# Reloads and values tied to TensorE, a third buffer for weight pieces, and a last tile in halves, in an attention and two-MoE kernel

## The chip, the cores and the metric

The kernel runs on one core of a Trainium2 chip. TensorE (PE) multiplies, VectorE (DVE) and ScalarE (ACT) work on elements, GpSimd (POOL) issues some transfers, and SyncE (SP) issues most of them, one after another in program order. The metric is the device time of one execution in microseconds (us), as the median of several executions.

## What is computed

```python
p_packed = sm_attn(p, k, v)            # 4 batches, 8 heads, 32 packed rows, 576 positions, 64 wide
out = sm_attn(q, p_packed, p_packed)   # softmax(scale * q @ k.T) @ v, the sum with 1e-9
x = out as 2304 tokens x 512
x = mish(x @ moe_w_in) @ moe_w_out     # 512 -> 2048 -> 512
x = elu(x @ moe2_w_in) @ moe2_w_out    # 512 -> 2048 -> 512
```

All data is f32. q, k and p are drawn eight times larger than v.

## The kernel before, in words

The matrix products run on pairs: a value is split into a high part (`gh`, `w1oh`) and the rest (`gl`, `w1ol`), and three products (high-high, high-low, low-high) make one. ACT writes the high part (`split_hi`), DVE the low part (`split_lo`).

**Startup** (`startup`, to about 125 us) takes the attention of batches 0 and 1 and the first 32 of the first MoE's 128 steps; its order is written out by hand in the string ORDER, for all engines. Behind it the framework's scheduler orders the instructions of each engine by priorities and its own estimate of times, within what the dependencies allow.

**`mixture1`** runs a loop over i = 32 to 129, a step per block of 288 tokens and 128 of the 2048 inner columns. Each step makes `gemm1(i)` (6 matmuls of 288 columns into a bank `h`), `mish(i)` on ACT and DVE, and `gemm2(i - 2)` (12 matmuls into `acc`). Between these the next batches advance in small steps from two queues: `att` (attention of batches 2 and 3: keys transposed on DVE, scores of the two halves s = 0 and 1 by `scores1`, softmax, transposes of the exponentials by `transpose_a1`, product with v by `packed`) and `fol`, the folds. `fold(b, c)` multiplies the first MoE's input weight, a quarter c, into the packed attention of batch b, so that batch b's `gemm1` needs no attention output. The decoded weight lies in DRAM (`w1_dr`, 8 pieces of 512 KB) and is read back by `reload_w1i(c)` into two tiles `w1r`c`_`h, five steps before the fold is due. Third, `step_w2` cuts the second MoE's input weight: raw words are loaded (`raw_w2i`), decoded by one step on ACT (L201) and three on DVE (L221, L231, L237), summed and differenced, and seven combined pieces `w2c` are split by ACT and DVE and written to DRAM by POOL (L326). They come back later for `mixture2`.

Two resources matter. PSUM's pool `ps_p` has one pair of banks, `pm`: after the startup each fold, each half of the scores and each transpose takes it in turn, and frees it when ACT and DVE have read it. And SP's transfers use eight semaphores in turn: a transfer of SP is issued only when the one eight places before it has landed.

**`mixture2`** runs three blocks j of 768 tokens. `quartet(j, q)` makes seven products of y and w2c in place of eight (p0 to p6, L833), with sums in `hs` and `r` on ACT and DVE and elu; `gemm4` adds up the second product in six banks (L913 to L915). `second(c)` and `tick(n)` feed the loads and decode of `w2o` into the same loop, n steps at a time.

`behind(ins)` puts an instruction after the last DVE instruction recorded so far, in the scheduler's order only (NoSync: nothing waits on the chip). The lines that the change touches: pool `wo` L109, `behind` L148, `reload_w1i` L336 to L343, `load_heads` L353, `transpose_a1` L495, `gemm4` L904, `attention_steps` L947, `second` L1113, `whole` L1137, the tick in `mixture2` L1262.

Of the kernel before, what the change touches and what calls it, by code (L numbers as in the profile page):

```python
# [72 lines left out]
def kernel(  # L73
# [32 lines left out]
    ptp = ctx.enter_context(tc.tile_pool(name="ptp", bufs=2))  # L106
    st = ctx.enter_context(tc.tile_pool(name="st", bufs=3))
    sg = ctx.enter_context(tc.tile_pool(name="sg", bufs=2))
    wo = ctx.enter_context(tc.tile_pool(name="wo", bufs=2))  # L109
    ps_a = ctx.enter_context(tc.tile_pool(name="ps_a", bufs=2, space=bass.MemoryType.PSUM))  # L110
    ps_h = ctx.enter_context(tc.tile_pool(name="ps_h", bufs=2, space=bass.MemoryType.PSUM))
    ps_p = ctx.enter_context(tc.tile_pool(name="ps_p", bufs=1, space=bass.MemoryType.PSUM))
# [32 lines left out]

    raws, halves, words = {}, {}, (deque(), deque())

    def behind(ins):  # L148
        last = next(
            (i for i in reversed(nc.cur_bb.bb.instructions) if i.engine == nc.vector.engine), None  # L150
        )
        if last is not None:
            tc.add_manual_dep(
                ins.ins, last.name,
                mybir.DependencyInfo(mybir.DependencyClass.NoSync, mybir.DependencyReason.DATA),
                reason="plan",
            )

# [178 lines left out]
    def reload_w1i(c, *which):  # L337
        for h in which or range(2):
            t = slot([128, 2, 512], F32, f"w1r{c}_{h}")
            ins = nc.sync.dma_start(out=t, in_=w1_dr[c * 2 + h])  # L340
            if which:
                behind(ins)
            w1v[c, h] = t  # L343


# [8 lines left out]
    def load_heads(src, dst, b, g, nm, eng):  # L354
        home = small if b else slot
        if nm == "v":
            t = home([128, 2, 5, D], F32, f"{nm}{b}_{g}")
            x = src[b, 2 * g:2 * g + 2].rearrange("h (p i) d -> p h (i d)", i=9)
            for r, j, n in RUNS:
                (eng if b or not j else nc.scalar).dma_start(  # L360
                    out=t[r:r + 64, :, 0:n, :].rearrange("p h i d -> p h (i d)"),
                    in_=x[:, :, D * j:D * (j + n)],
                )
        elif b == 0 or nm == "k" and b == 1:

            t = home([128, S // 32, 32], F32, f"{nm}{b}_{g}")
            ins = eng.dma_start(
                out=t.rearrange("p c d -> p (c d)"),
                in_=src[b, 2 * g:2 * g + 2].rearrange("h (t j) d -> (h t) (j d)", t=64),
            )  # L370
            if b == 1:
                tc.keep_in_program_order(ins)
        else:
            t = home([128, S // 32, 32], F32, f"{nm}{b}_{g}")
            for h in range(2):
                for x in range(2):
                    r = 64 * h + 32 * x
                    if nm == "q":
                        eng.dma_start(
                            out=t[r:r + 32],  # L380
                            in_=src[b, 2 * g + h, :, 32 * x:32 * x + 32].rearrange("(c t) d -> t c d", t=32),
                        )
                    for s in range(2 if nm == "k" else 0):
                        eng.dma_start(
                            out=t[r:r + 32, s * NB // 2:(s + 1) * NB // 2, :],
                            in_=src[b, 2 * g + s, h * HALF:(h + 1) * HALF, 32 * x:32 * x + 32].rearrange(
                                "(c t) d -> t c d", t=32
                            ),
                        )
        dst[b, g] = t  # L390
# [96 lines left out]
    def transpose_a1(b, s, eng):  # L487
        d = {}

        def pe():  # L490
            e1 = E1.pop((b, s))
            ps = d["ps"] = pm()
            for i, w, bank, x in CHUNKS:
                i0 = i * 128
                nc.tensor.transpose(  # L495
                    out=ps[bank][0:w, x * 128:(x + 1) * 128], in_=e1[:, i0:i0 + w], identity=ident
                )

        def post(eng=eng):
            a1 = small([128, len(CHUNKS), 128], F32, f"a1t{b}_{s}")  # L500
            for bank in range(2):
                mine = [c for c in CHUNKS if c[2] == bank]
                w, i0, n = mine[0][1], mine[0][0], len(mine)
                evac(
                    eng, a1[0:w, i0:i0 + n, :],
                    d["ps"][bank][0:w, 0:n * 128].rearrange("p (c x) -> p c x", x=128),
                )
            A1T[b, s] = a1

        return [pe, post]  # L510
# [391 lines left out]
    def gemm4(j, kk, half):  # L902
# [4 lines left out]
        gh, gl = gt2.pop((j, kk, half))  # L907
        wh, wl = (x[:, kk % 2, :] for x in wt["w2o", kk // 2])
        n = count[j, half] = count.get((j, half), 0) + 1
        for t in range(3):  # L910
            ts = slice(t * 128, (t + 1) * 128)
            o = acc[j][3 * half + t]
            nc.tensor.matmul(out=o, lhsT=gh[:, ts], rhs=wh, start=(n == 1), stop=False)  # L913
            nc.tensor.matmul(out=o, lhsT=gh[:, ts], rhs=wl, start=False, stop=False)  # L914
            nc.tensor.matmul(out=o, lhsT=gl[:, ts], rhs=wh, start=False, stop=(n == NK))  # L915
        if n == NK:
            for t in range(3):
                o = acc[j][3 * half + t]
# [4 lines left out]
                else:  # L923
                    ob = slot([128, 512], F32, "ob")
                eng = nc.gpsimd if j < 2 else (nc.sync, nc.scalar)[t % 2]
                evac("av"[t % 2], ob, o)
                a = 2 * HN * j + HN * half + t * 128

                r = 0
                while r < 128 and a + r < S:  # L930
# [16 lines left out]
    def attention_steps(b):  # L947
# [9 lines left out]
        st = [transpose_heads(kt_in, kT, b, g, "kT") for g in range(4)]  # L957
        for s in range(2):
            pe, top, expo, sums = scores1(b, s)
            st.append([then(pe, lambda: load_vt(b, 0), lambda: load_vt(b, 1)) if s else pe, lambda top=top, expo=expo: (top(), expo()), sums])  # L960
        st += [transpose_a1(b, s, P["EVA"][s]) for s in range(2)]
        for s in range(2):
            pe, scaled, turn, out = packed(b, s)
            st.append([then(pe, lambda s=s: load_kt(q, qt_in, b, s, "q")), scaled, lambda turn=turn, out=out: (turn(), out())])
# [20 lines left out]
    def startup():  # L985
# [15 lines left out]
        if WARM:  # L1001
            wu = ps_h.tile([128, 512], F32, tag="h", name="warm")

            one = const.tile([128, 128], F32R, name="one")
            nc.gpsimd.tensor_copy(out=one, in_=ident)

            def busy():
# [104 lines left out]

    def second(c):  # L1113
        rows = [4 * c + r for r in (0, 2, 1, 3)]
        for r in rows[:2]:
            todo.append(lambda r=r: load_raw("w2o", r, 0))
        for x, r in enumerate(rows):
            d = []

            def step(i, r=r, d=d):  # L1120
                if not d:
                    d.extend(decode("w2o", r, 0))
                d[i]()

            todo.extend(lambda i=i, step=step: step(i) for i in range(6))
            if x < 2:
                todo.append(lambda r=rows[x + 2]: load_raw("w2o", r, 0))

    def tick(n):
        while n and todo:  # L1130
# [3 lines left out]
    def mixture1():  # L1134
        att, fol = Track(), Track()

        def whole(f):  # L1137
            return [f[0], lambda: [f[i]() for i in (1, 3, 2, 4)]]

        at = {}  # L1140

# [93 lines left out]
    def mixture2():  # L1235
        ready = deque()
        for j in range(3):
            for q in range(NQ):
# [13 lines left out]
                for x in range(7):  # L1252
# [4 lines left out]
                    if x in (0, 2, 4, 6):  # L1257
                        if x == 6:
                            ready.append(groups[0])
                        if ready:  # L1260
                            gemm4(*ready.popleft())
                    tick(4 if lastq else 2)  # L1262
                ready.extend(groups[1:])
        while ready:
            gemm4(*ready.popleft())
# [37 lines left out]
```

## Time and profile before

| | |
|---|---|
| runs | 778.14, 778.45 and 782.45 us, median 778.45 |
| profiled execution | 775.32 us, of which the span from the first to the last instruction is 773.5 |
| busy | PE 756.9 us (98%), DVE 528.7 (68%), ACT 397.6 (51%), POOL 104.5 (14%) |
| DMA | 138.82 MB, 179 GB/s on average |
| largest groups | L833 198.1 us, L737 to L739 148.7 to 151.2 each, L913 to L915 101.1 to 113.5 each, all PE |

A matmul's busy time overlaps that of its neighbour, so a PE that is busy without a gap issues a 288-column matmul every 0.13 us though each is shown with 0.29. Line numbers are those of the kernel before; after the change they are two to five higher in the functions named here, and more from `gemm4` on.

### The profile page before, as it was taken

The numbers are of one execution on the slowest core, as the hardware profiler recorded it, in microseconds if no ns is written. First come the engines' busy times: TensorE is split into PE (matmuls) and PEld (weight loads), VectorE is DVE, ScalarE is ACT, GpSimd is POOL, SyncE is SP. The second block draws the span as 40 slices with busy tenths as digits, with TensorE's granted clock in tenths as the row PEclk, the third lists the DMA queues.
The fourth block names the chain that finished last, engine by engine and source line by source line (L and its number), as shares of the span: only waits on it lengthen the run. The fifth ranks groups of instructions, "written<-read, shape, count | busy, mean of one in ns | idle before, by whom it ended". The sixth has DMA issues, their size and how long they took to land.

```text
span 773.5 us, 14181 instructions
## 1 busy us (share of the span) xinstructions
PE 756.9 (98%) x5276; PEld 679.0 (88%) x5276; DVE 528.7 (68%) x1132; ACT 397.6 (51%) x843; POOL 104.5 (14%) x199
## 2 busy tenths in 40 slices
PE   8899999999999999999999999999999999999997
PEld 6598898898889988999988889888998999899986
DVE  5999977735853679877667788866455686445554
ACT  3899826573657467665545344534323354223323
POOL 1100000120120215661000003133000001000000
PEclk9999999999999999999999999999999999999999
DMA  8998646685583555777666235456343347333312
GB/s 290 412 367 271 171 126 177 203 230 157 129 268 56 151 194 191 262 254 238 219 220 201 100 109 199 155 197 198 108 120 119 103 140 243 108 110 116 129 55 82
DMA packets 95108, 138.82 MB, mean 179 GB/s; under 512 B 57920, under 2 KB 63616, under 8 KB 95040
## 3 DMA queue, kind: packets, MB, share of 16 engines
q1 hardware_dynamic: 83104, 105.73, 44.1%
q0 software_dynamic: 10208, 29.90, 10.6%
q10 hardware_dynamic: 1728, 2.29, 0.9%
q8 instruction: 42, 0.69, 0.3%
q14 instruction: 26, 0.21, 0.1%
HBM read 109.58 MB, written 28.31 MB: 178 GB/s over the span
## 4 chain that ended last, share of the span: by engine, by line
PE 84%; ACT 6%; DVE 4%; DMA 3%; issue 2%; POOL 0%; SPq 0%; ACTq 0%; DVEq 0%; POOLq 0%
PE h L833 22%; PE o L913 8%; PE o L915 8%; PE o L914 8%; PE acc L738 7%; PE acc L737 7%; PE acc L739 7%; PE h L701 3%; PE h L702 3%; PE h L703 3%; DMA raw_w1o<-in_moe_w_out_dram 1%; PE pm L667 1%; PE pm L520 1%; DMA w_dr<-w2c 1%; ACT words L206 1%
## 5 line engine op out<-in xcount | busy, mean ns | idle before, releaser
L833 PE MATMUL h<-y,w2c 128*128 128x384 f32 x1008 | 198.1, 338 | 1.8 <-ACT hs L397 1.2
L833 PEld LDWEIGHTS h<-y,w2c 128*128 128x128 f32 x1008 | 179.5, 188 | 13.4 <-ACT hs L397 2.0
L738 PE MATMUL acc<-gl,w1oh 128*128 128x288 f32 x512 | 151.2, 296 | 0.4 <-DVE gl L719 0.3
L739 PE MATMUL acc<-gh,w1ol 128*128 128x288 f32 x512 | 150.3, 295 | 0.0
L737 PE MATMUL acc<-gh,w1oh 128*128 128x288 f32 x512 | 148.7, 296 | 0.2 <-ACT gh L397 0.2
L913 PE MATMUL o<-w2oh,gh 128*128 128x512 f32 x288 | 113.5, 394 | 0.0
L914 PE MATMUL o<-w2ol,gh 128*128 128x512 f32 x288 | 112.6, 391 | 0.0
L915 PE MATMUL o<-w2oh,gl 128*128 128x512 f32 x288 | 101.1, 393 | 0.0
L738 PEld LDWEIGHTS acc<-gl,w1oh 128*128 128x128 f32 x512 | 96.1, 188 | 5.3 <-issue 2.3
L737 PEld LDWEIGHTS acc<-gh,w1oh 128*128 128x128 f32 x512 | 95.0, 188 | 6.2 <-issue 4.5
L739 PEld LDWEIGHTS acc<-gh,w1ol 128*128 128x128 f32 x512 | 96.0, 188 | 1.2 <-issue 0.8
L719 DVE TENSOR_TENSOR gl<-t,gh 128x288 fp32r<-128x288 f32 x128 | 57.2, 451 | 43.3 <-ACT gh L397 42.4
L711 ACT ACTIVATE t<-h 128x288 f32<-128x288 f32 x128 | 51.0, 404 | 55.9 <-PE h L703 53.0
L701 PE MATMUL h<-a2h,gh 128*128 128x288 f32 x256 | 76.9, 301 | 1.3 <-ACT t L711 0.9
L326 POOL DMA_DIRECT2D w_dr<-w2c x112 | 59.7, 539 | 135.7 <-DVE w2c L272 126.9
L703 PE MATMUL h<-a2h,gl 128*128 128x288 f32 x256 | 76.1, 298 | 0.3 <-DVE gl L272 0.3
L702 PE MATMUL h<-a2l,gh 128*128 128x288 f32 x256 | 75.8, 296 | 0.0
L264 ACT ACTIVATE gh<-t 128x384 fp32r<-128x384 f32 x96 | 50.1, 522 | 48.8 <-DVE t L844 47.5
L270 DVE TENSOR_TENSOR gl<-t,gh 128x384 fp32r<-128x384 f32 x96 | 53.1, 554 | 15.8 <-ACT gh L264 15.4
L914 PEld LDWEIGHTS o<-w2ol,gh 128*128 128x128 f32 x288 | 54.1, 188 | 9.4
L913 PEld LDWEIGHTS o<-w2oh,gh 128*128 128x128 f32 x288 | 54.0, 187 | 9.4 <-ACT gh L264 0.5
L397 ACT ACTIVATE gh<-t 128x288 fp32r<-128x288 f32 x112 | 49.2, 442 | 24.1 <-PE acc L739 22.1
(139 smaller groups left out, 1095.2 us busy)
## 6 DMA issues: line engine op xcount, KB each, us to landing
w2c<-w_dr SPq DMA_DIRECT2D x84, 512.0 KB, 3.6
w_dr<-w2c POOLq DMA_DIRECT2D x112, 128.0 KB, 3.1
w1r<-w_dr SPq DMA_DIRECT2D x24, 512.0 KB, 5.7
raw_w1i<-in_moe_w_in_dram SPq DMA_DIRECT2D x16, 512.0 KB, 10.8
raw_w1o<-in_moe_w_out_dram SPq DMA_DIRECT2D x16, 512.0 KB, 9.1
raw_w2i<-in_moe_w_in_dram SPq DMA_DIRECT2D x16, 512.0 KB, 4.8
raw_w2o<-in_moe_w_out_dram SPq DMA_DIRECT2D x16, 512.0 KB, 3.6
y_dr<-y POOLq DMA_DIRECT2D x16, 288.0 KB, 4.9
```

What stands on the lines that cost most here:

```text
L326: nc.gpsimd.dma_start(out=w2_dr[n // 2][:, n % 2, p], in_=d[x][:, i].bitcast(F32))
L701: nc.tensor.matmul(out=hp, lhsT=wh, rhs=xh, start=(kt == 0), stop=False)
L702: nc.tensor.matmul(out=hp, lhsT=wh, rhs=xl, start=False, stop=False)
L703: nc.tensor.matmul(out=hp, lhsT=wl, rhs=xh, start=False, stop=(kt == 1))
L719: nc.vector.tensor_tensor(out=gl, in0=d["t"], in1=gh.bitcast(F32), op=ALU.subtract)
L737: nc.tensor.matmul(out=o, lhsT=wh[:, cs], rhs=gh, start=first, stop=False)
L738: nc.tensor.matmul(out=o, lhsT=wh[:, cs], rhs=gl, start=False, stop=False)
L739: nc.tensor.matmul(out=o, lhsT=wl[:, cs], rhs=gh, start=False, stop=last)
L833: nc.tensor.matmul(out=hp, lhsT=w[:, p, a, :], rhs=y[:, b, :], start=start and p == 0 and i == 0, stop=p == 1 and i == 2, skip_group_check ...
L913: nc.tensor.matmul(out=o, lhsT=gh[:, ts], rhs=wh, start=(n == 1), stop=False)
L914: nc.tensor.matmul(out=o, lhsT=gh[:, ts], rhs=wl, start=False, stop=False)
L915: nc.tensor.matmul(out=o, lhsT=gl[:, ts], rhs=wh, start=False, stop=(n == NK))
```

## The change

1. The pool `wo` (pieces `w2c` while they are written out, and `r` of `quartet`) has three buffers.
2. `behind` takes an engine and can make a real wait. A reload of `mixture1` (called without `which`) waits on the chip for the last PE instruction recorded; so do the eight loads of v of each of the batches 2 and 3.
3. v is loaded in two parts, one behind the scores of each half. Transposes of half 1 of the batches 2 and 3 stand behind the last PE instruction in the scheduler's order, and for batch 2 half 0 gets three empty steps.
4. The fold's copies run high, high, low, low (before: high, low, high, low).
5. The tile `one` of the startup comes from another pool.
6. `second` loads w2o two decode steps earlier and the next group's first rows ahead; `tick` takes three steps instead of two in the quartets 0 to 5 of the first block.
7. The last output tile is multiplied, copied and stored in two halves of 256 columns.

```diff
     sg = ctx.enter_context(tc.tile_pool(name="sg", bufs=2))
-    wo = ctx.enter_context(tc.tile_pool(name="wo", bufs=2))
+    wo = ctx.enter_context(tc.tile_pool(name="wo", bufs=3))
...

-    def behind(ins):
+    def behind(ins, eng=nc.vector, wait=False):
         last = next(
-            (i for i in reversed(nc.cur_bb.bb.instructions) if i.engine == nc.vector.engine), None
+            (i for i in reversed(nc.cur_bb.bb.instructions) if i.engine == eng.engine and i.name != ins.ins.name), None
         )
         if last is not None:
             tc.add_manual_dep(
                 ins.ins, last.name,
-                mybir.DependencyInfo(mybir.DependencyClass.NoSync, mybir.DependencyReason.DATA),
+                mybir.DependencyInfo(
+                    mybir.DependencyClass.Sync if wait else mybir.DependencyClass.NoSync, mybir.DependencyReason.DATA
+                ),
                 reason="plan",
             )

...
         for h in which or range(2):
             t = slot([128, 2, 512], F32, f"w1r{c}_{h}")
             ins = nc.sync.dma_start(out=t, in_=w1_dr[c * 2 + h])
-            if which:
-                behind(ins)
+            behind(ins, nc.vector if which else nc.tensor, not which)
...
             t = home([128, 2, 5, D], F32, f"{nm}{b}_{g}")
             x = src[b, 2 * g:2 * g + 2].rearrange("h (p i) d -> p h (i d)", i=9)
             for r, j, n in RUNS:
-                (eng if b or not j else nc.scalar).dma_start(
+                ins = (eng if b or not j else nc.scalar).dma_start(
                     out=t[r:r + 64, :, 0:n, :].rearrange("p h i d -> p h (i d)"),
                     in_=x[:, :, D * j:D * (j + n)],
                 )
+                if b > 1:
+                    behind(ins, nc.tensor, True)
...
             ps = d["ps"] = pm()
             for i, w, bank, x in CHUNKS:
                 i0 = i * 128
-                nc.tensor.transpose(
+                ins = nc.tensor.transpose(
                     out=ps[bank][0:w, x * 128:(x + 1) * 128], in_=e1[:, i0:i0 + w], identity=ident
                 )
+                if b > 1 and s and not i:
+                    behind(ins, nc.tensor)
...
         n = count[j, half] = count.get((j, half), 0) + 1
+
+        def products(t, cs, skip):
+            ts = slice(t * 128, (t + 1) * 128)
+            o = acc[j][3 * half + t][:, cs]
+            nc.tensor.matmul(out=o, lhsT=gh[:, ts], rhs=wh[:, cs], start=(n == 1), stop=False, skip_group_check=skip)
+            nc.tensor.matmul(out=o, lhsT=gh[:, ts], rhs=wl[:, cs], start=False, stop=False, skip_group_check=skip)
+            nc.tensor.matmul(out=o, lhsT=gl[:, ts], rhs=wh[:, cs], start=False, stop=(n == NK), skip_group_check=skip)
+
+        final = n == NK and j == 2 and not half
+        cuts = [slice(0, 256), slice(256, 512)]
         for t in range(3):
-            ts = slice(t * 128, (t + 1) * 128)
-            o = acc[j][3 * half + t]
-            nc.tensor.matmul(out=o, lhsT=gh[:, ts], rhs=wh, start=(n == 1), stop=False)
-            nc.tensor.matmul(out=o, lhsT=gh[:, ts], rhs=wl, start=False, stop=False)
-            nc.tensor.matmul(out=o, lhsT=gl[:, ts], rhs=wh, start=False, stop=(n == NK))
+            for cs in cuts if final and t == 2 else [slice(0, 512)]:
+                products(t, cs, cs.start is not None and cs.start > 0)
         if n == NK:
             for t in range(3):
                 o = acc[j][3 * half + t]
...
                 else:
                     ob = slot([128, 512], F32, "ob")
                 eng = nc.gpsimd if j < 2 else (nc.sync, nc.scalar)[t % 2]
+                a = 2 * HN * j + HN * half + t * 128
+                if final and t == 2:
+                    for x, cs in enumerate(cuts):
+                        evac("av"[x], ob[:, cs], o[:, cs])
+                        (nc.scalar, nc.sync)[x].dma_start(out=out[a:a + 128, cs], in_=ob[:, cs])
+                    continue
                 evac("av"[t % 2], ob, o)
-                a = 2 * HN * j + HN * half + t * 128
...
         st = [transpose_heads(kt_in, kT, b, g, "kT") for g in range(4)]
         for s in range(2):
             pe, top, expo, sums = scores1(b, s)
-            st.append([then(pe, lambda: load_vt(b, 0), lambda: load_vt(b, 1)) if s else pe, lambda top=top, expo=expo: (top(), expo()), sums])
+            st.append([then(pe, lambda s=s: load_vt(b, s)), lambda top=top, expo=expo: (top(), expo()), sums])
         st += [transpose_a1(b, s, P["EVA"][s]) for s in range(2)]
+        if b == 2:
+            st[-2] += [lambda: None] * 3
         for s in range(2):
...
-            one = const.tile([128, 128], F32R, name="one")
+            one = tp.tile([128, HN], F32R, tag="t", name="one")[:, 0:128]
...

     def second(c):
         rows = [4 * c + r for r in (0, 2, 1, 3)]
-        for r in rows[:2]:
+        ahead = rows[2:] + [r + 4 for r in rows[:2] if 0 < c < 3]
+        for r in rows[:2 if c < 2 else 0]:
             todo.append(lambda r=r: load_raw("w2o", r, 0))
         for x, r in enumerate(rows):
             d = []
...
                     d.extend(decode("w2o", r, 0))
                 d[i]()

-            todo.extend(lambda i=i, step=step: step(i) for i in range(6))
-            if x < 2:
-                todo.append(lambda r=rows[x + 2]: load_raw("w2o", r, 0))
+            todo.extend(lambda i=i, step=step: step(i) for i in range(4))
+            for n in ahead[x:x + 1]:
+                todo.append(lambda n=n: load_raw("w2o", n, 0))
+            todo.extend(lambda i=i, step=step: step(i) for i in range(4, 6))

...
         att, fol = Track(), Track()

         def whole(f):
-            return [f[0], lambda: [f[i]() for i in (1, 3, 2, 4)]]
+            return [f[0], lambda: [g() for g in f[1:]]]

...
-                    tick(4 if lastq else 2)
+                    tick(4 if lastq else 3 if j == 0 and q < 6 else 2)
```

Where rows move, three places. SP's queue at the end of the startup (k2 are the keys of batch 2, w1r1 to w1r3 the reloads for batch 1's folds, raw_w2i the second MoE's first rows), before:

```order
L384 DMA k2_0_1930<-in_k_dram 32x9x32 x6
L340 DMA w1r1_0_1918<-w1_dr2_141 128x1024
L340 DMA w1r1_1_1920<-w1_dr3_142 128x1024
L340 DMA w1r2_0_1922<-w1_dr4_143 128x1024
L340 DMA w1r2_1_1924<-w1_dr5_144 128x1024
L340 DMA w1r3_0_1926<-w1_dr6_145 128x1024
L340 DMA w1r3_1_1928<-w1_dr7_146 128x1024
L384 DMA k2_0_1930<-in_k_dram 32x9x32 x2
L384 DMA k2_1_1939<-in_k_dram 32x9x32 x8
L384 DMA k2_2_1948<-in_k_dram 32x9x32 x8
L384 DMA k2_3_1957<-in_k_dram 32x9x32 x8
L162 DMA raw_w2i0_0_2000<-in_moe2_w_in_dram 128x1024
```

And after:

```order
L387 DMA k2_0_1930<-in_k_dram 32x9x32 x8
L342 DMA w1r1_0_1918<-w1_dr2_141 128x1024
L342 DMA w1r1_1_1920<-w1_dr3_142 128x1024
L342 DMA w1r2_0_1922<-w1_dr4_143 128x1024
L342 DMA w1r2_1_1924<-w1_dr5_144 128x1024
L342 DMA w1r3_0_1926<-w1_dr6_145 128x1024
L342 DMA w1r3_1_1928<-w1_dr7_146 128x1024
L387 DMA k2_1_1939<-in_k_dram 32x9x32 x8
L387 DMA k2_2_1948<-in_k_dram 32x9x32 x8
L387 DMA k2_3_1957<-in_k_dram 32x9x32 x8
L164 DMA raw_w2i0_0_2000<-in_moe2_w_in_dram 128x1024
```

Two k2 loads moved ahead of the reloads; 24 stand behind them, and now behind the reloads' wait on PE. Further on, four loads of v2 moved ahead of the fourth w2i row and the next reloads.

On DVE, between the keys' transposes and the maximum of the scores of batch 2, half 0 (`gl1_3` is the low part of the last fold of batch 1, `dec` the decoding of raw_w2i), before:

```order
L272 SCALAR_TENSOR_TENSOR w2c_2369<-dec_2051,w2c_2369 128x2x128
L237 SCALAR_TENSOR_TENSOR dec_2187<-raw_w2i1_0_2002,dec_2187 128x512
L289 TENSOR_TENSOR sums_2285<-dec_2051,dec_2187 128x256
L272 SCALAR_TENSOR_TENSOR gl1_3_2098<-pm_2059,gh1_3_2097 128x512
L289 TENSOR_TENSOR sums_2285<-sums_2285,dec_2051 128x256
L289 TENSOR_TENSOR dec_2051<-dec_2051 128x256
L272 SCALAR_TENSOR_TENSOR gl1_3_2098<-pm_2059,gh1_3_2097 128x512
```

And after:

```order
L223 TENSOR_SCALAR dec_2051<-raw_w2i0_0_2000 128x512
L233 SCALAR_TENSOR_TENSOR dec_2051<-raw_w2i0_0_2000,dec_2051 128x512
L223 TENSOR_SCALAR dec_2187<-raw_w2i1_0_2002 128x512
L239 SCALAR_TENSOR_TENSOR dec_2051<-raw_w2i0_0_2000,dec_2051 128x512
L233 SCALAR_TENSOR_TENSOR dec_2187<-raw_w2i1_0_2002,dec_2187 128x512
L274 SCALAR_TENSOR_TENSOR gl1_3_2098<-pm_2059,gh1_3_2097 128x512 x2
L274 SCALAR_TENSOR_TENSOR w2c_2369<-dec_2051,w2c_2369 128x2x128
```

`gl1_3` moved ahead of the pieces and sums, and stands directly behind five decoding steps. ACT has the same picture: its steps on raw_w2i0 and raw_w2i1 (L203) stand directly ahead of the two copies `gh1_3`.

On PE the scores of batch 2, half 0, and what stands around them, before (they begin at PE's row 908):

```order
L701 MATMUL h1_2344<-a2h1_1885,gh1_2_2053 128x288
L431 MATMUL pm_2243<-kT2_3_2215,pD_102 32x288 x2
L431 MATMUL pm_2243<-kT2_2_2185,pD_102 32x288 x2
L431 MATMUL pm_2243<-kT2_1_2157,pD_102 32x288 x2
L431 MATMUL pm_2243<-kT2_0_2128,pD_102 32x288 x2
```

And after (from row 891):

```order
L707 MATMUL h1_2297<-a2l1_1886,gh1_2_2053 128x288
L434 MATMUL pm_2243<-kT2_3_2215,pD_102 32x288 x2
L434 MATMUL pm_2243<-kT2_2_2185,pD_102 32x288 x2
L434 MATMUL pm_2243<-kT2_1_2157,pD_102 32x288 x2
L434 MATMUL pm_2243<-kT2_0_2128,pD_102 32x288 x2
```

They moved 17 rows towards the front, from the gemm1 that makes `h1_2344` into the one before it; the scores of half 1 moved by as many. The fold with w1r1 moved from row 763 to row 769.

## Rows read from the trace of the kernel before

**Rows 1.** The page's first part: span; an engine's busy us, share, instructions.

```profile
span 773.5 us, 14181 instructions
PE 756.9 (98%) x5276; PEld 679.0 (88%) x5276; DVE 528.7 (68%) x1132; ACT 397.6 (51%) x843; POOL 104.5 (14%) x199
```

**Rows 2.** PE's waits, 100 us to the end: line, releaser, us, times, longest.

```profile
PE h L833 <- ACT hs L397: 1.2, 2, 0.6
PE pm L495 <- ACT e L468: 0.5, 1, 0.5
PE h L833 <- DVE t L844: 0.4, 1, 0.4
PE acc L738 <- DVE gl L719: 0.3, 1, 0.3
PE h L833 <- DVE r L895: 0.2, 1, 0.2
PE acc L737 <- ACT gh L397: 0.2, 1, 0.2
```

**Rows 3.** Windows: length; PE, PEld, DVE, ACT, POOL busy; clock; DMA; GB/s.

```profile
20.00:40.00 20.00, 16.05 (x97) 11.04 (x96) 19.55 (x46) 16.59 (x31) 2.73 (x4) 1.00 1.02 412
...
150.00:170.00 20.00, 19.47 (x169) 17.99 (x168) 8.73 (x25) 14.64 (x32) 6.41 (x12) 1.00 0.92 283
```

**Rows 4.** Timeline of SP's queue: start us, us, engine, line, transfer, count.

```profile
111.10 12.08 SPq L340 DMA_DIRECT2D w1r<-w_dr  x6
123.23 14.31 SPq L384 DMA_DIRECT2D k<-in_k_dram  x26
137.66 10.06 SPq L162 DMA_DIRECT2D raw_w2i<-in_moe_w_in_dram  x4
150.77 9.02 SPq L360 DMA_DIRECT2D v<-in_v_dram  x8
```

**Rows 5.** Line L340, the reloads: ns to issue (min/median/max); time to landing.

```profile
L340 SPq DMA_DIRECT2D w1r<-w_dr x24: 319/380/1078, 46.1 to 282.7; - x24
...
DMA to landing us min/median/max: 3.2/5.7/9.7
```

**Rows 6.** Timeline of PE, five places (start, length, matmuls run together).

```profile
124.63 0.29 PE L703 MATMUL h<-a2h,gl 128*128 128x288 f32 x1
...
130.39 1.09 PE L667 MATMUL pm<-w1r,pt 64*32 64x512 f32 x16
...
152.34 0.71 PE L431 MATMUL pm<-kT,pD 64*32 64x288 f32 x16
...
158.45 0.72 PE L431 MATMUL pm<-kT,pD 64*32 64x288 f32 x16
...
173.28 0.90 PE L520 MATMUL pm<-v,a1t 128*32 128x64 f32 x40
```

**Rows 7.** Timeline of ACT around the first w2i rows and the softmax.

```profile
141.84 0.68 ACT L201 ACTIVATE raw_w2i<-raw_w2i 128x512 f32<-128x512 f32 x1 [0.43 <-DMA raw_w2i<-in_moe_w_in_dram]
...
148.41 0.60 ACT L264 ACTIVATE gh<-pm 128x512 fp32r<-128x512 f32 x1 [1.39 <-DVE gl L272]
...
154.85 1.28 ACT L468 ACT_TABLE_LOAD   x1
...
156.66 0.47 ACT L468 ACTIVATE e<-pm,sm 128x256 f32<-128x256 f32 x1
```

**Rows 8.** Timeline of DVE in the same stretch.

```profile
143.02 0.69 DVE L231 SCALAR_TENSOR_TENSOR dec<-raw_w2i,dec 128x512 int32<-128x512 int32 x1
...
149.04 0.69 DVE L272 SCALAR_TENSOR_TENSOR gl<-pm,gh 128x512 fp32r<-128x512 f32 x1
...
153.16 0.76 DVE L455 TENSOR_REDUCE sm<-pm 128x1 f32<-128x576 f32 x1 [1.05 <-PE pm L431]
```

**Rows 9.** Page, DMA issues: transfer, queue, count, size, median us to landing.

```profile
w_dr<-w2c POOLq DMA_DIRECT2D x112, 128.0 KB, 3.1
```

**Rows 10.** Timeline of DVE at the end of the span.

```profile
768.92 0.69 DVE L399 COPY ob<-o 128x512 f32<-128x512 f32 x1 [1.55 <-ACT ob L397]
```

## The prediction

> **What bounds the kernel now.** I read the page's first part, then the waits of TensorE (PE) after the startup, then the windows, and last the timelines of SP, PE, ACT and DVE around 110 to 165 us. The page says that PE is busy 756.9 of 773.5 us [rows 1]. The reader should see in the waits that after 100 us PE waits for a named releaser only seven times, 2.8 us together, and never longer than 0.6 us at once [rows 2]. So no edit after the startup can win more than about 2.8 us (0.36%), while an edit that makes PE wait costs its full length. The startup is written out by hand and the diff leaves its order alone, so I count nothing before 108 us. One window shows slack that is not there elsewhere: 150 to 170 us has PE at 19.47 of 20.00 [rows 3]. There the scores of batch 2 share one PSUM pair (`pm`) with the last fold of batch 1, and it is the stretch that the new waits reach first.
>
> **The gate on the reloads.** In before, SP issued six reloads of w1 (512 KB each) from 111.10 us, then 26 loads of k2, then the first w2i rows at 137.66 [rows 4]. Now the first reload waits for the last PE instruction recorded ahead of it, the last matmul of `gemm1(31)`, L703 at 124.63 + 0.29 [rows 6]; call it 125.0. Behind it on SP stand the other reloads, 24 k2 loads, and raw_w2i0 and 1. A reload takes SP 0.38 us to issue and lands after 3.2 us at best, 5.7 at the median, 9.7 at worst [rows 5]. Six together are 3.15 MB. At the best rate a window shows, 412 GB/s [rows 3], each takes 1.27 us of the engines: the first lands at 128.2, the second at 129.5, the sixth at 134.6. The first fold that reads them stood at 130.39 [rows 6], and six matmuls later now (131.2), so it does not wait, with 1.7 us to spare.
>
> The Trainium skill, "DMA: Bandwidth & Descriptors", section Specifications, gives a core about 358 GB/s of HBM; by it each reload would take 1.46 us, the sixth would land at 135.5, and the sum below would be 0.9 us larger; the trace's 412 GB/s decides. The Trainium skill, the same page, section Rules for kernel authors, says to issue a DMA early and to wait for it late; that speaks against a gate like this one, and by it the loss that follows is the price.
>
> Each DMA of SP waits for the one eight before it. So the third to eighth load of k2_1 go out as reloads one to six land, the last at 134.6. Sixteen k loads are left, at 14.31/26 = 0.55 us each [rows 4]: they end at 143.4, 5.9 us later than before. raw_w2i0 goes out at 143.5. From its issue to ACT's first touch took 137.66 to 141.84, 4.2 us [rows 4, 7]: now 147.7. raw_w2i1 follows 0.4 us behind and, by the same engine time of 1.3 us, lands near 148.7.
>
> **First stall.** The order now puts ACT's step on raw_w2i1 ahead of both `gh1_3` copies, and DVE's five decode steps ahead of both `gl1_3`. In before they stood beside data that had landed. ACT: 148.7 + 0.68 = 149.4, then two copies of 0.60 [rows 7] to 150.5. DVE: 147.7 + 0.68 on ACT, then five steps of 0.4 to 0.69 [rows 8], 2.7 together, to 151.1; then two `gl` of 0.69 to 152.35. Only then is `pm` free. PE wants it for the scores of half 0, which stand 17 rows (0.133 us each) ahead of where they stood: 152.34 - 2.26 = 150.1 [rows 6]. **PE waits 2.2 us.** Bounds: nothing, if all six reloads land as the quickest one did (125.0 + 5 x 0.42 + 3.2 = 130.3, which moves all of this 4.3 us earlier); 4.4 us, if the last takes 9.7 (127.1 + 9.7 = 136.8). I take the value between because six in a row can't each have the engines alone, and nothing stands ahead of them; by the median alone the sixth would land at 127.1 + 5.7 = 132.8 and the stall be 0.4.
>
> **Second stall.** After `gl1_3` DVE has ten steps of about 0.4 us (four of them of w2c, three sums) before the maximum of half 0 (0.76 [rows 8]): 152.35 + 4.0 + 0.8 = 157.1, with the scaling 157.5. ACT has a fourth w2c piece ahead of the table load, and three buffers: it waits for the first piece's write, issued near 153.3, median 3.1 us to land [rows 9]: 156.4. Then three ACT steps (1.2), the table load 1.28, two exponentials (0.98) [rows 7]: 159.9. PE wants `pm` for half 1 at 158.45 - 2.26 + 2.2 = 158.4 [rows 6]. **PE waits 1.5 us.** Bounds: 0.5 if the write is not what ends last (DVE's 157.5, a softmax step already loaded, 0.4 + 0.98 to 158.9); nothing if the sixth reload comes 3.8 us earlier, since all of this hangs on `gl1_3`; 3.0 if the write lands 1.5 us late. The 0.5 that PE waits now at L495 [rows 2] I leave as it is.
>
> **The clock.** PE idled 4 of 20 us between 20 and 40 us and the granted clock stayed 1.00 [rows 3], so the stalls cost their own length.
>
> **Values behind PE.** The eight loads of v2 start at 150.77 [rows 4]. Four now wait for the scores of half 0 and four for those of half 1, near 152.8 and 159. Queued behind them on SP are a raw_w2i row, two reloads and q2. Their first reader, the product with v, stands at 173.28 [rows 6], 13 us after the last issue, longer than the slowest reload took to land [rows 5]. Cost nothing; if that cover went, a microsecond or two, which I put into the upper end. Batch 3 is the same with no stall near it. The transposes tied behind PE and the three empty steps move work that PE does anyway: nothing.
>
> **Fold copies together.** ACT's second copy waited 1.39 us for DVE's `gl` of the first [rows 7]; now ACT runs both and DVE follows. It shortens the hold of `pm` by about 0.9 us per fold, and is already inside the PE order that I use (scores 17 rows earlier). It buys nothing by itself where PE did not wait.
>
> **Third buffer, w2o two steps earlier, three ticks.** These act from 360 us on, where PE's waits are hs 1.2 (two), t 0.4 and r 0.2 [rows 2]. The third buffer also serves `r`; steps of the decode leave DVE and ACT at other times. Which waits go can't be read from the rows: the most is 1.8 us, the least nothing, and a new wait of one step (0.6) is as possible. I take the wait for r and one of the two for hs: **-0.8 us**.
>
> **Tail.** The last tile is copied by ACT and DVE in halves. But the copy that ends last is another one: DVE's copy of 768.92, which waited 1.55 us for ACT's read of its PSUM pair [rows 10], and its store is issued after it. The diff doesn't touch it; the halves add three small matmuls. Nothing, within 0.4 either way.
>
> **Sum.** +2.2 + 1.5 - 0.8 = +2.9 us on the profiled execution of 775.3, that is 778.2. The runs' median of 778.45 lies 3.1 above that execution, so I forecast 781.3.
>
> **Rivals.** (1) *The gated loads stay hidden.* It needs the sixth reload by 132.4 for the first stall and by 130.8 for both. For it: the quickest reload lands in 3.2 us and the median alone would give 132.8; and the engines' room is there, with 283 of 412 GB/s used even in 150 to 170 us [rows 3]. Against it: the six queue behind each other. Then only the later waits change: -0.8 us, 777.7. (2) *Backlog, the other sign by more.* The decode of w2i is late by 6 us while PE goes on, so DVE and ACT carry both it and the softmax of batch 2. If the last reload takes 9.7 us, stall one is 4.4 us; if w2c's writes are late, stall two is 3.0 more, and the late v and raw_w2i cost two: +8.6 us, 787.1. It decides from a sixth reload at about 136. Against it: nothing else in this stretch loads the engines as the startup did. (3) *The change only removes waits, and the new order hides more than I see*: 2.8 us at most, 775.7, by the waits [rows 2].
>
> **How the numbers follow.** Forecast (a loss of 0.5 to 5.5 us): 0.60. Rival 1 with rival 3: 0.27. Rival 2: 0.13. The forecast's own range is 779 to 784. To leave out no more than 2 in 10, the range takes in rival 1 down to 775.5 and most of rival 2 up to 786.5. One per cent, about what a measurement of this kernel can tell from no change, is 7.8 us: 770.7 and 786.2. No case reaches the lower one (0.02 for what I don't see); of rival 2 about two thirds pass the upper one (0.09); the rest is 0.89.
>
> **What would show it.** In the profile after: SP's first gated reload at 125.0 (right) or not; last k2 load near 143.4 and raw_w2i0 near 143.5; a PE wait at the scores of batch 2 with DVE `gl` (L274) as its releaser, 2.2 us, and one with ACT `e` (L471) near 158 us, 1.5 us; no wait at L520 or at a fold of w1r; hs and r shorter after 400 us; the last store issued by ACT at an unchanged distance from PE's end. The prediction is wrong if 125 to 165 us shows PE busy within 1 us of 40, since the whole loss is there, or if PE waits somewhere that isn't named here.

## The result, and the profile after

| | before | after |
|---|---|---|
| median of the runs taken together | 778.14 us (5 runs) | 786.92 us (5 runs, 785.5 to 787.68) |
| ratio, 95% interval | | 1.0107 (1.0084 to 1.0130) |
| profiled execution, its span | 775.32, 773.5 | 787.14, 785.1 |
| PE busy | 756.9 us | 762.2 us |

The change costs 8.8 us, 1.1%. The forecast of 781.3 had the sign and not the size, and the upper end of its range, 786.5, is 0.4 short.

The windows of the kernel after, in the columns of [rows 3]:

```profile
20.00:40.00 20.00, 17.62 (x107) 12.64 (x93) 18.64 (x44) 15.50 (x28) 2.42 (x4) 0.83 1.02 413
...
125.00:150.00 25.00, 22.18 (x184) 18.77 (x184) 11.22 (x21) 9.36 (x23) 1.08 (x2) 0.96 0.67 188
150.00:170.00 20.00, 17.17 (x144) 15.77 (x143) 13.51 (x32) 11.86 (x26) 5.33 (x10) 0.96 0.74 244
```

From 125 to 170 us PE is idle 5.65 us, and the granted clock, the column after POOL, is below 1.00. In before the second of these windows lacked 0.53 us and the clock stood at 1.00 [rows 3]. What PE waits for, from 126 to 180 us:

```profile
PE pm L672 <- issue: 2.8, 1, 2.8
PE pm L434 <- DVE gl L274: 1.7, 1, 1.7
PE pm L498 <- ACT e L471: 1.2, 1, 1.2
PE pm L434 <- ACT e L471: 1.1, 1, 1.1
```

The two at L434, the scores of batch 2, are the two forecast stalls. The first row is not among them: L672 is the fold that reads w1r3. "issue" names no releaser; the DVE rows further down show what it waited for. SP's queue, where the gate is:

```profile
109.57 3.94 SPq L387 DMA_DIRECT2D k<-in_k_dram  x8
126.39 2.78 SPq L342 DMA_DIRECT2D w1r<-w_dr  x6
129.22 19.27 SPq L387 DMA_DIRECT2D k<-in_k_dram  x24
148.60 7.57 SPq L164 DMA_DIRECT2D raw_w2i<-in_moe_w_in_dram  x3
158.52 2.56 SPq L361 DMA_DIRECT2D v<-in_v_dram  x4
```

SP stands still from 113.5 to 126.4 us. Its waits have the row, and the reloads' line says how long they then took to land:

```profile
SPq L342 <- PE h L708: 12.8, 1, 12.8
```

```profile
DMA to landing us min/median/max: 3.3/5.0/10.5
```

This execution left the startup 1.4 us later than the one of before (the first k2 load 109.57 against 108.17); without that the gate opened at 125.0, as forecast. raw_w2i0 went out at 148.60 in place of 137.66 [rows 4]: 9.5 us later without the 1.4, where 5.9 had been worked out.

### The profile page after: what moved, and what is told of

It is laid out like the page before. It is cut to its first block, busy times and chain, and to the rows that moved or that the text cites. A ratio compares the mean times of both kernels' runs of the same rounds, so it can differ in the third digit from the quotient of the medians.

```text
span 785.1 us, 14224 instructions
## 1 busy us (share of the span) xinstructions
PE 762.2 (97%) x5279; PEld 682.3 (87%) x5279; DVE 531.0 (68%) x1133; ACT 400.4 (51%) x845; POOL 104.5 (13%) x199
## 3 DMA queue, kind: packets, MB, share of 16 engines
q0 software_dynamic: 10208, 29.90, 10.5%
## 4 chain that ended last, share of the span: by engine, by line
PE 65%; DMA 10%; ACT 9%; DVE 8%; issue 4%; SPq 2%; POOL 1%; ACTq 0%; DVEq 0%; POOLq 0%
PE h L838 21%; PE o L919 8%; PE o L921 8%; PE o L920 8%; PE acc L742 4%; PE acc L743 4%; PE acc L744 4%; DMA k<-in_k_dram 2%; DMA w_dr<-w2c 2%; SPq L387 2%; PE h L706 2%; PE h L708 2%; PE h L707 2%; DMA raw_w2o<-in_moe_w_out_dram 2%; DMA raw_w2i<-in_moe_w_in_dram 1%
## 5 line engine op out<-in xcount | busy, mean ns | idle before, releaser
L743 PE MATMUL acc<-gl,w1oh 128*128 128x288 f32 x512 | 151.6, 297 | 0.4 <-DVE gl L724 0.2
L919 PE MATMUL o<-w2oh,gh 128*128 128x512 f32 x289 | 113.7, 393 | 0.5 <-ACT gh L266 0.4
L919 PEld LDWEIGHTS o<-w2oh,gh 128*128 128x128 f32 x289 | 54.2, 188 | 10.2 <-ACT gh L266 1.2
L921 PEld LDWEIGHTS o<-w2oh,gl 128*128 128x128 f32 x289 | 53.8, 188 | 8.9
```

Source lines behind the costliest of these rows:

```text
L743: nc.tensor.matmul(out=o, lhsT=wh[:, cs], rhs=gl, start=False, stop=False)
L919: nc.tensor.matmul(out=o, lhsT=gh[:, ts], rhs=wh[:, cs], start=(n == 1), stop=False, skip_group_check=skip)
L921: nc.tensor.matmul(out=o, lhsT=gl[:, ts], rhs=wh[:, cs], start=False, stop=(n == NK), skip_group_check=skip)
```

## The experiments

All are versions of the changed kernel unless said. Two theories at the start: **A**, the gate makes late what stands behind it on SP, and PE waits for that; **B**, the new order of the engines costs by itself. A third, **C**, came up as the narrow form of A was tried: the reloads themselves, 3 MB moved late and at once, are what is late. Ratios are to the kernel before, run beside each.

**Without the gate.**

```diff
-            behind(ins, nc.vector if which else nc.tensor, not which)
+            if which:
+                behind(ins)
```

> The changed kernel, but the reloads of the fold weights in the first mixture wait for nothing again (all other parts stay). Theory A (the gate holds SP's queue, and what stands behind it is late): SP issues the first reloads near 111 us and raw_w2i0 near 138 us, PE's stalls of 2.8, 1.7 and 1.1 us between 145 and 166 us go, the granted clock stays at its upper level there, and the time falls by 7 to 9 us to about 778 (ratio to the kernel before 0.997 to 1.003). Theory B (the new order of the engines, which comes from the fold copies, three buffers and values, costs the time by itself): the stalls stay in part, and the time is above 782.

777.59 us, 1.0008 (0.9987 to 1.0030). The only wait of PE from 126 to 180 us, and SP's queue:

```profile
PE h L707 <- ACT t L717: 0.4, 1, 0.4
```

```profile
111.75 12.06 SPq L342 DMA_DIRECT2D w1r<-w_dr  x6
123.86 14.29 SPq L388 DMA_DIRECT2D k<-in_k_dram  x26
138.27 7.57 SPq L164 DMA_DIRECT2D raw_w2i<-in_moe_w_in_dram  x3
```

The whole loss is the gate's, and everything else in the change together is worth nothing that shows. B falls as the cause of the loss; what a new order adds beside a gate is seen further down.

**The gate alone, in the kernel before** (the same line, and the new `behind`).

> The kernel before, with one thing of the change: the reloads wait for the last TensorE instruction. Theory A: the whole loss comes with it, 785 to 788 us (ratio 1.009 to 1.013), with a stall of more than 2 us at the fold that reads w1r3 and raw_w2i0 issued after 145 us. Theory B: 778 to 781.

787.97 us, 1.0132 (1.0086 to 1.0178); raw_w2i0 goes out at 146.79. PE waited 4.1 us at the scores for the softmax and 3.3 at `acc` for `gl`, not at the fold, where theory A had put the stall. The gate makes the loss in another order too; where the stall shows depends on the order.

**Keys first.** The k2 loads are recorded ahead of the gated reloads.

```diff
+        for x in range(2):
+            at[2 * NK].append(lambda x=x: load_kt(k, kt_in, 2, x, "k"))
...
-                for x in range(2):
+                for x in range(2 if b > 2 else 0):
```

> The changed kernel with the 32 loads of k2 recorded ahead of the gated reloads, so that they stand in front of the waiting instruction on SP. Theory A in its narrow form (the lateness of k2, and of the DVE transposes that stand ahead of the fold's low parts, makes the long stall): the reloads still go out at about 125 us, but land in 8 to 10 us, the stall at the fold of w1r3 (2.8 us) and the low clock after it go, raw_w2i0 is issued near 129 us, and the time is 777 to 780. If the reloads themselves are what comes too late (theory C): the stall stays, PE waits at the fold of w1r3 or w1r2 for a reload, and the time stays above 783.

786.44 us, 1.0111 (1.0066 to 1.0155): no gain. SP's queue and PE's longest waits:

```profile
109.95 17.43 SPq L387 DMA_DIRECT2D k<-in_k_dram  x32
127.54 2.77 SPq L342 DMA_DIRECT2D w1r<-w_dr  x6
130.42 14.90 SPq L164 DMA_DIRECT2D raw_w2i<-in_moe_w_in_dram  x3
```

```profile
PE h L706 <- ACT t L716: 2.8, 3, 1.8
PE pm L434 <- ACT e L471: 2.5, 1, 2.5
```

The stall at the fold and the low clock went, as A in its narrow form had it, and the price stayed. With reloads from 127.5 us on, all three folds came late: ACT's copies of the first began at 140.47, where in the kernel without the gate they began at 132.22. PE did not wait for that fold: its two reloads had landed at 131.22 and 132.42, and it ran at 139.27, because the scheduler had put it 48 matmuls further back in PE's order than in the kernel after.

```profile
139.27 1.09 PE L672 MATMUL pm<-w1r,pt 64*32 64x512 f32 x16
```

raw_w2i0, issued at 130.4, lay behind six reloads in the DMA queue and reached ACT at 142.33, between two folds; `gemm1` waited for ACT's `t`, and the softmax of half 0 came 2.5 us late. So late keys are one way to lose, and late reloads, with folds planned later and rows behind them, another.

**Keys first, no gate.** The two edits above together; SP's own pace puts the reloads at 125 us.

> The 32 keys' loads ahead of the reloads as in the run with the keys first, but no wait of the reloads on TensorE. SP needs 0.5 us per key load, so the reloads go out near 126.5 us by SP's pace alone, a microsecond earlier than with the gate. If lateness from whatever cause is what costs (theory C), the loss stays: 784 to 787, with raw_w2i0 landing behind 3 MB of reloads near 141. If the wait itself costs: 777 to 779.

785.00 us, 1.0103 (1.0069 to 1.0137), with no wait of the reloads on PE, the folds in the same places of PE's order, and as late (ACT's first copies at 138.72). The wait itself costs little or nothing; reloads that go out at 125 in place of 111, with the rows behind them and the order planned for them, cost this, whatever holds them.

**Rows first.** raw_w2i0 and 1 are loaded ahead of the keys and the gate.

```diff
-        at[2 * NK] = [late_p]
+        at[2 * NK] = [late_p, lambda: [load_raw("w2i", r, 0) for r in range(2)]]
...
-                        load_raw("w2i", *ahead.popleft())
+                        ahead.popleft()
```

> The changed kernel with the first two rows of the second MoE's weight loaded ahead of the keys and the gated reloads (near 105 us). It takes one of the two late things away and leaves the other. Theory A (the late keys make the stall of 2.8 us at the fold of w1r3 and the low clock after it, the late rows make the stalls at the scores): the fold's stall stays, the stalls of 1.7 and 1.1 us at the scores go or halve, 781.5 to 784.5. If the fold's stall alone carries the loss: 786 and more. If the rows alone: below 779.5.

781.05 us, 1.0045 (1.0026 to 1.0063). From 126 to 180 us one wait of PE is left:

```profile
PE pm L672 <- issue: 3.1, 1, 3.1
```

Both stalls at the scores are gone, and the fold's stays. With the low clock behind it, it is about the 3.4 us that remain.

**Keys and rows first.** Both edits, with the gate.

> The changed kernel with both the keys and the first two rows ahead of the gated reloads: nothing that anyone needs soon stands behind the gate, and the six reloads go out near 127 us as in the run with the keys first. If the price of the gate is what stands behind it on SP and in the DMA queue: the loss goes, 776.5 to 779.5, with no stall at the fold of w1r3. If the reloads themselves come too late for the folds: a stall of PE at the folds of w1r2 or w1r3 with a transfer as its releaser, 781 and more.

779.08 us, 1.0024 (1.0008 to 1.0040). No stall at a fold or at the scores; three of 0.4 to 1.1 us at `h` remain, the first for `gh` of the late fold. The folds are as late as with the keys first (ACT's first copies at 140.00), and 1.4 us are left. As there, the first fold's place is the scheduler's: it ran at 138.80, its second reload had landed at 131.24, and PE did not wait for it. C, late reloads with the order planned for them, is worth 1.4 us; whether the transfers or the order make it was not separated. The other 7 us come from what stood behind the reloads: keys in front of a fold's copies on DVE, and rows whose decoding then met folds and softmax on ACT and DVE.

**The gate earlier**, on the 60th PE instruction before, and on the 30th (a count `back` in `behind`, for these six reloads alone).

> The changed kernel, its gate on the six reloads tied to the 60th TensorE instruction ahead of the one it waited for, some 8 us earlier. If the loss is the lateness of what stands behind the gate (theory A), the first four reloads go out near 117 us and land by 127, the last two wait for their buffers until 122.4 as in the kernel before, raw_w2i0 goes out near 138, and the loss is gone: 777 to 779.5. If a wait of SP on TensorE costs by being there, or by what the scheduler makes of it: above 783.

> The same with 30 instructions, some 4 us earlier than the changed kernel's gate (near 121 us). Theory A as a chain with slack: the sixth reload lands near 134 instead of 138 (counted from a gate at 125), the keys end 4 us earlier, the 2.8 us stall at the fold of w1r3 shrinks to nothing and the others by half or more: 778 to 781.5, clearly less than half of the loss. As a chain without slack, 4 of 9 us would come back: 782 to 784.

**The gate on the last pair.**

```diff
-            behind(ins, nc.vector if which else nc.tensor, not which)
+            if which or c == 3:
+                behind(ins, nc.vector if which else nc.tensor, not which)
```

> The changed kernel with the gate on the last two reloads (w1r3) alone; the four for w1r1 and w1r2 go out near 111 us as in the kernel before. The last two had to wait for their buffers until 122.4 there, and go out at 125 now. If what costs is that 2 MB of reloads are moved from an idle stretch (111 to 121 us) into the busy one (theory C): keys and raw_w2i only 2 to 3 us late, 777.5 to 780. If any wait behind which the keys stand costs the same (theory A in its narrow form): above 783.

Eight microseconds earlier: 778.38, 1.0011 (0.9992 to 1.0029). The ten times spread from 775.94 to 783.93 and the profiled one is the longest, so its rows are not used in the table. In that execution raw_w2i0 went out 3.8 us late, not on time as expected, and PE waited 1.7, 1.3, 1.3 and 1.1 us; what the other nine did, no trace shows. Four: 783.62, 1.0075 (1.0055 to 1.0094). The last pair: 781.54, 1.0053 (1.0033 to 1.0072), above what C and below what A gave it. raw_w2i0's issue, counted from each execution's first k2 load, against the loss:

| kernel | first k2 load | raw_w2i0 issued | late by | loss |
|---|---|---|---|---|
| no gate | 108.81 | 138.27 | 0.0 | 0.2 |
| last pair | 108.51 | 140.92 | 2.9 | 3.9 |
| 30 earlier | 109.21 | 143.74 | 5.0 | 6.0 |
| after | 109.57 | 148.60 | 9.5 | 8.8 |

(29.5 us in before; the loss is median less median.) No gate and last pair have the same order of instructions on PE, DVE and ACT, and of transfers on SP and POOL, from end to end: they differ by the wait alone, which makes raw_w2i0 2.9 us later and costs 3.7 us. PE's waits with the last pair, where no gate has 0.4 us:

```profile
PE pm L499 <- ACT e L472: 2.0, 1, 2.0
PE h L707 <- ACT t L717: 0.9, 1, 0.9
PE pm L435 <- DVE gl L274: 0.2, 1, 0.2
```

The gates 60 and 30 instructions earlier share one order too, and their medians lie 5.2 us apart for 4 us of gate. The other versions were scheduled anew, so the table as a whole is a trend: the chain has no slack that shows, and each microsecond of lateness costs about one, from the first 3 us on. In the kernel with 30 earlier the stalls at the scores are 1.3 each though the reloads had gone out at 122.

**No wait of the values on PE.**

```diff
-                if b > 1:
-                    behind(ins, nc.tensor, True)
```

> The changed kernel without the waits of the loads of v on TensorE (the split of these loads in two parts stays). My prediction put them at nothing: 786 to 787.5 us, the same as the changed kernel. The rival, that raw_w2i and the reloads queued behind the waiting v loads cost 1 to 2 us: 784 to 785.

790.60 us, 1.0157 (1.0120 to 1.0194): slower than the kernel after by 3.7, which neither side had (four times from 789.03 to 791.44, against 785.5 to 787.68). PE's waits from 126 to 180 us, and ACT's row behind the first:

```profile
PE pm L432 <- ACT e L469: 5.0, 1, 5.0
PE pm L670 <- issue: 3.2, 1, 3.2
PE pm L432 <- DVE gl L274: 1.7, 1, 1.7
```

```profile
165.00 0.42 ACT L266 ACTIVATE w2c<-sums 128x256 fp32r<-128x256 f32 x1 [4.97 <-DMA w_dr<-w2c]
```

The fourth w2c piece waits for the first one's write to DRAM, and the softmax stands behind it on ACT. Here that wait is 4.97 us; in the kernel after it is 0.95. Without the waits the first four loads of v go out at 148.6 us (158.5 in the kernel after), and the fourth w2i row and the other four loads from 157.9 us on (161.25 and 165.8); these share the DMA queue with those writes. With the rows late, holding v back is worth 3.7 us; that it is the sharing, and not the new order, the rows suggest and no run separates.

**The rest of the change alone**: no gate, no wait and no split of v, no ordered transposes, no empty steps.

> The changed kernel without any wait on TensorE and without the values' split, the transposes' order and the empty steps: three buffers, fold copies together, w2o earlier, three ticks and the tail in halves remain. My prediction gave these -0.8 us in sum: ratio 0.998 to 1.000, 776 to 777.5. If they bring nothing: the same as the kernel without the gate, ratio 1.000 to 1.002. If the waits of v help also where nothing is late, this kernel is slower than the one without the gate by over 1 us.

777.80 us, 1.0006 (0.9988 to 1.0024): three buffers, folds together, earlier w2o, ticks and tail bring nothing that shows, and with nothing late the waits of v don't either (777.59 with them).

**Rows first, no gate.**

> The changed kernel without the gate, and with the first two rows of the second MoE's weight loaded ahead of the reloads: nothing near 150 us is late, and the 0.5 to 0.7 us that TensorE waited there in the kernel before may go. If those waits were all that is left to win here: 776.5 to 777.7, ratio 0.998 to 1.000, the only version of this study that could pass the kernel before. If the earlier rows push the decode into a full stretch of DVE: 778 to 780.

776.89 us against 778.37, 0.9982 (0.9970 to 0.9993). Its windows:

```profile
125.00:150.00 25.00, 25.00 (x212) 21.99 (x212) 19.86 (x41) 14.14 (x34) 3.29 (x7) 1.00 0.75 218
150.00:170.00 20.00, 20.00 (x174) 18.74 (x174) 7.71 (x21) 14.46 (x31) 5.29 (x10) 1.00 0.73 195
```

The half microsecond that before lacked from 150 to 170 [rows 3] is there. This version is 0.2% below the kernel before, the only one of the twelve whose whole interval is below 1; a difference so small, found once among twelve, is a hint and not a result.

## Why the prediction was right or wrong

**Right: the gate.** Its time (125.0 without the startup's 1.4), that SP's queue behind it is the price, the two stalls at the scores (2.2 and 1.5 forecast, 1.7 and 1.1 measured), and that v behind PE, the transposes and the tail cost nothing that shows. The tail: DVE's copy again waits for ACT's read of its PSUM pair, 1.55 us as in [rows 10]; the half tile behind it in this row now ends last, and the store issued last is SP's, not ACT's as forecast. From the start of PE's last matmul to the end it is 5.1 us, and 5.2 before.

```profile
780.52 1.02 DVE L402 COPY ob<-o 128x512 f32<-128x512 f32 x2 [1.55 <-ACT ob L400]
```

The Trainium skill, "DMA: Bandwidth & Descriptors", section Rules for kernel authors, has the rule that spoke against the change, to issue early and wait late. The trace agrees: 8.8 us for a gate that held six reloads 14 us back, 0.8 us (-0.6 to 2.3) for one 8 us earlier.

**Wrong: "the sixth at 134.6".** It landed 12.9 us after the gate and not 9.6: issued at 128.77, it took the 10.5 us of the reloads' line. I gave each reload the 1.27 us of the best window. What the DMA engines did from 126 to 144 us, in slices of 0.45 us (busy tenths, GB/s):

```profile
DMA  0009699999898999998988899999991245444434
GB/s 0 0 0 146 264 382 419 410 410 392 310 400 328 428 401 401 373 319 246 273 237 218 302 349 386 400 395 297 201 155 42 46 62 81 72 78 80 74 64 68
```

Up to 139.5 us they are busy nine tenths of the time, but move 218 to 302 GB/s in the middle. Two writes of y, 288 KB each, went out on POOL there (L763); I had left them out of the sum. The sixth reload was as slow with the keys out of the way (landed 13.1 us after the first was issued, in the kernel with keys and rows first), so it is not the keys. By their bytes alone, at 412 GB/s [rows 3], the two writes would be worth 1.4 of the 3.3 us that are missing, by estimate. That it is the writes was not tried.

**Right by its rate, with a meaning I had missed: the keys.** Sixteen keys took 9.2 us (8.8 forecast). In the last ten slices of that row the engines are one to five tenths busy, at 42 to 81 GB/s: what sets the pace is SP, half a microsecond to issue each 36 KB. The gate did not only move 3 MB; it left SP idle for 12.8 us in front of 12 us of issuing. (In before SP stood still too, for 8.3 us, but with four of the six reloads already out.)

The Trainium skill, the same page, section Issuing engines are not separate DMA queues, calls the sequencer's time to start a DMA usually small next to the DMA itself. For these keys the trace shows it as the limit: each takes 2.2 us from issue to landing (the median), but SP starts only one in half a microsecond, and the DMA engines are not full.

**Wrong: no wait "at a fold of w1r".** This is the largest part that was missing. I followed the keys to raw_w2i and not to their own transposes, though in DVE's order kT2_1 and kT2_2 stand ahead of the fold's `gl1_2`:

```profile
137.31 0.78 DVE L412 STREAM_TRANSPOSE kT<-k 128x576 f32<-128x576 f32 x1
141.63 0.78 DVE L412 STREAM_TRANSPOSE kT<-k 128x576 f32<-128x576 f32 x1 [3.54 <-DMA k<-in_k_dram]
145.58 0.78 DVE L412 STREAM_TRANSPOSE kT<-k 128x576 f32<-128x576 f32 x1 [3.17 <-DMA k<-in_k_dram]
146.28 1.25 DVE L274 SCALAR_TENSOR_TENSOR gl<-pm,gh 128x512 fp32r<-128x512 f32 x2
```

DVE waits for keys twice, then frees `pm` at 147.5, and PE's next fold starts at 147.63: the stall of 2.8 us. It is not the fold's own weight, whose last reload had landed at 139.3. The prediction named a wait at a place that it doesn't name as a sign of being wrong, and this is one.

**Wrong: "the stalls cost their own length".** PE after that stall:

```profile
147.63 1.46 PE L672 MATMUL pm<-w1r,pt 64*32 64x512 f32 x16 [2.82 <-issue]
...
149.67 0.44 PE L742 MATMUL acc<-gh,w1oh 128*128 128x288 f32 x1
149.91 0.44 PE L743 MATMUL acc<-gl,w1oh 128*128 128x288 f32 x1
...
151.59 0.33 PE L742 MATMUL acc<-gh,w1oh 128*128 128x288 f32 x1
```

Matmuls start 0.24 us apart in place of 0.13, and the fold takes 1.46 in place of 1.09 [rows 6]: the clock stood at its lower level, 1.2 GHz, until 151.6. Some ten matmuls and the fold, 1.5 us more. I had read one window at 1.00 with idle PE as proof that a stall leaves the clock alone.

**Wrong: -0.8 us from 360 us on.** The wait for hs fell from 1.2 to 0.6, but waits of 0.4 (L919 for `gh`) and others came, and the kernel with the rest of the change alone shows no gain.

**The sum of after.** 2.8 + 1.5 for the fold and the clock, 1.7 + 1.1 at the scores, 0.7 more at L498 than before: 7.8 us between 126 and 180 us, of a loss of 8.8 by the medians. The two profiled executions lie 11.6 us apart, 1.4 of it from the startup, so 2.4 us of that pair are not in this list. Rival 2 came nearest: it put its turning point at a sixth reload at 136, and the sixth came at 137.9 without the startup's 1.4. But its parts were others, the fold and the clock in place of late writes and v.

One step of the first stall's sum is a tenth off (151.1 and two `gl` of 0.69 make 152.5, not 152.35), which changes nothing.

What stays open: why the middle of the reloads moved slowly, and the single hold at which the loss begins. The steps of the table are 3 us wide.

## What to carry to other kernels

A wait put on a queue's instruction is a wait for all that stands behind it: count what follows until the next idle stretch, in issuing time as well as in bytes, and follow each late tile to the first instruction of every engine that stands in front of others, not only to the one that is known to be critical. In a kernel that is 98% one engine such a wait can win little, and here it lost about a microsecond for each by which it made the urgent loads late; put it only where nothing urgent stands behind, or move the urgent loads ahead. A stall of the matrix engine can also lower its clock; here 1.5 us came on top of 2.8 that way.

## What the runs showed of the hardware

- PE's clock. After a wait of 2.82 us the granted clock was at its lower level until 151.6, while PE worked without a gap from 147.63 on; after one of 3.06 (rows first) it fell as well, and the fold took 1.96 us. After the wait of 2.49 us with the keys first it stayed at its upper level: the scores took 0.72 us, as in [rows 6].
- The startup ended 0 to 1.8 us later from one profiled execution to the next (first k2 load 108.1 to 109.95 us), though its order on PE, DVE and ACT is the same in all. In the kernel after, the clock from 20 to 40 us was 0.83, and matmuls near 38 us stood 0.24 us apart; in before it was 1.00 [rows 3]. The two need not go together: the gate alone had 0.91 and its first k2 load at 108.13. Such a difference has to be taken off before two traces are compared. It is not all that executions of one kernel differ by: the kernel before ranged from 775.21 to 780.41 us in one series.
